# A hand-ordered attention-and-gated-MLP block on one core: w_phi loaded first, nearly all loads on one queue, and a new order of work

## The chip, the core and the metric

The kernel runs on one core of one Trainium2 chip. The time is the device time of one execution in microseconds (us). Three runs of the kernel before give 271.66 to 272.04 us, with a median of 271.83 us.

## What is computed

Two pre-normalised layers over one sequence of 2048 rows and 640 columns, in bf16. The first is linear attention with 32 heads of 20 columns and a softmax feature map; the second is a gated product of two projections.

```python
x = A_x
h = x + _A_ref(_layernorm(x), A_wqkv, A_w_phi, A_wo)
h2 = h + _B_ref(_layernorm(h), B_w_gate, B_w_up, B_w_down)

# _A_ref
pq, pk = q @ w_phi[head], k @ w_phi[head]
phi_q = concat([softmax(pq), softmax(-pq)]);  phi_k = concat([softmax(pk), softmax(-pk)])
kv = phi_k^T v;  z = sum(phi_k);  o = (phi_q kv) / (phi_q z + 1e-6);  return o @ wo
# _B_ref
return ((x @ w_gate) * (x @ w_up)) @ w_down
```

## The kernel before

The 2048 rows are 16 tiles t of 128 rows. Every step of the program is a named operation, recorded by `G.op(engine, name, ...)`, and the table `PLAN` gives each name a key, an alternative engine and its buffer slots. `arrange` sorts by the key, so each engine's instruction list is written out in full by the table. `emit` adds the semaphore waits. An engine runs its list strictly in order: what waits holds up all that stands behind it. The names used below are these.

- Loads (line 285): `x0` to `x14` bring x (x4, x6, x8 and so on bring two tiles, 320 KB), `w5` brings w_phi (25 KB), `wk0` to `wk4` and `wv0` to `wv4` the key and value parts of wqkv (160 KB each). `wo`, `wd`, `wg`, `wu` bring the later weights, mostly 480 KB. `wqt0` to `wqt4` (line 309) bring the query part of wqkv by DMA transposes. All are issued by SP, or by ACT.
- Preparation of the weights: `zero` (DVE) and `warm` (PE, lines 367 and 372, products of zeros), `Ph0` to `Ph2` (POOL, line 380: w_phi spread out in the tensor Phi), `WT` (PE transposes of `wk`, line 392) with their copies `WTe`, and the folds `F1_i` and `F0_i` (PE, line 411: w_phi folded into the key and the query weights) with their copies `Fe` into the tensor Wp. All such copies out of PSUM have line 251.
- Normalisation of tile t: `L1s` (DVE, lines 428 and 429) and `L1a` (431) take statistics, `L1l` and `L1e` (ACT, 436 and 439) make the scale, `L1n` its product with the mean, and `xn` (453) the normalised tile. It is transposed by PE for tiles 0 and 1 (`xt`, line 462) and by the DMA queue of SP for the others (line 471).
- Projections (PE, line 482): `V`, `K` and `Q` of tile t. The first two tiles are cut into five parts, `K0_0` to `K0_4`, so that each part waits for one piece of the folded weights alone. Features: `Kx`, `Qx` (ACT, exponentials), `Ks`, `Qs` (DVE, lines 498 and 556, sums), `Kr`, `Ke`, `Qr`, `Qe` (ACT, logarithm and exponential), `Kn`, `Qn` (POOL, lines 518 and 570, scaling), and `Qb` (line 563), the subtraction of the two logarithms of a query's sums, on DVE or POOL. `qT` is the DMA transpose of the query features.
- Attention: `KV` (PE, line 526) sums up over all tiles, `N` (588) is the numerator, `dd`, `rd`, `o` (DVE) divide, `oT` is a DMA transpose, and `O` (625) multiplies with wo. `h` (DVE, 631) adds x. `hc` and the DMA transpose `hT` prepare the second layer.
- Second layer: `U` (PE, line 668) the two projections in blocks of rows, `g` (ACT) and `u` (DVE) their product, `D` (687) the product with w_down, `y` (DVE, 699) the sum with h, and the store.

The kernel's own filler on PE is set by two lines, which say how many zero products there are, and which of them have to precede the first transposes:

```python
NFILL = 14
wall = [G.by["warm%d" % k] for k in range(8)]
```

Of the kernel before, what the change touches and what calls it, by code (L numbers as in the profile page):

```python
# [47 lines left out]
NFILL = 14  # L48
# [5 lines left out]
x1:0.78:1 ekz:0.78 x0:0.78 zero:0.91 id0:1.014 warm0:1.127 id1:1.252 x3:1.26:1 wk3:1.26:1 warm1:1.345 va1:1.496 warm2:1.564 w5:1.74:1 warm3:1.782 warm4:2.001  # L54
warm5:2.219 wk0:2.22:1 eps:2.326 gl0:2.357 warm6:2.437 gla:2.518 warm7:2.656 wk4:2.7:1 glb:2.822 warm8:2.874::0 warm9:3.093 wk1:3.18 warm10:3.311 warm11:3.529
wk2:3.66:1 L1s1:3.725 warm12:3.748 warm13:3.966 x4:4.14 warm14:4.185 warm15:4.403 L1s0:4.512 wv1:4.62 warm16:4.621 warm17:4.84 wv0:5.1:1 L1a1:5.299 L1s3:5.408
WT3:5.446::1 L1l1:5.532 wv2:5.58:1 Ph2:5.775 L1e1:5.858 warm18:5.902 warm19:6.011 wv3:6.06 WTe3:6.1:1 warm20:6.12 L1a0:6.195 xn1:6.304::0 Ph1:6.369 x2:6.54
WT0:6.546::2 L1l0:6.685 Ph0:6.761 L1a3:6.834 xt1:6.971::3 wv4:7.02:1 WTe0:7.023:1 L1l3:7.067 L1e0:7.249 WT4:7.25::4 L1e3:7.393 xte1:7.486 xn0:7.487::1 x6:7.5
L1n3:7.673 WT1:7.746::5 phz:7.897 WTe4:8.017:1 warm21:8.025 F1_0:8.134::6 WTe1:8.223:1 xn3:8.425::2 F1_3:8.453::0 WT2:8.772::2 Fe1_0:8.808:1 xt0:9.051::3
xt3:9.063 WTe2:9.249:1 F1_1:9.33::4 Fe1_3:9.392 F1_4:9.649::6 xte0:9.657:1 Fe1_1:9.976 L1s4:10.065 F1_2:10.153::0 x8:10.373 K0_0:10.472::2 Fe1_2:10.67:1  # L60
K0_1:10.743 L1s5:10.852 wqt4:10.853 K1_0:11.014::4 Fe1_4:11.254:1 K1_1:11.285 K1_2:11.556 L1a4:11.639 L1a5:11.762 V1_0:11.827::0 L1l4:11.995 K1_3:12.098
wqt1:12.163 L1s2:12.225 L1e4:12.321 V0_0:12.369::6 K1_4:12.64 V1_1:12.911 L1n5:13.012:1 Kx1_0:13.11::0 V0_1:13.182 xn5:13.296::3 V0_2:13.453 Kx1_1:13.694
V0_3:13.724 L1a2:13.826 xt5:13.934 L1s7:13.935 V0_4:13.995 K0_2:14.266 L1l2:14.278 K0_3:14.537 L1e2:14.604 Ve0:14.697::0 Ks1:14.722::0 V1_2:14.808 L1n2:14.884
V1_3:15.079 Sz:15.108 wqt0:15.244 xn2:15.281:1:0 L1n4:15.287 V1_4:15.35 K3:15.621::4 L1s6:16.115 Kr1:16.234 Ke1:16.525 xt2:16.554 x12:16.671:1 Kn1:16.859
K0_4:16.977 L1a6:17.025 xn4:17.134::1 Kx3_0:17.177::1 V3:17.248::6 L1s8:17.664 Kx3_1:17.761 wqt2:17.864 Ve1:18.345::1 L1a7:18.451 L1s9:18.56 K5:18.604::4
L1l6:18.929 xt4:19.174 L1e6:19.255 Ks3:19.347::1 Ve3:19.348::2 L1n7:19.535 L1n6:19.759 Kx0_0:19.932::2 V5:19.96::0 rqz:19.983 wqt3:20.484 Kx0_1:20.516
xn7:20.74::2 Kx5_0:21.1::3 xn6:21.27::3 K2:21.316::6 Kx5_1:21.684 L1a8:21.8 xt6:21.908 L1a9:21.909 Ks0:22.018::2 Kr3:22.268 Ke3:22.559 V2:22.672::2
Ve5:22.705::3 Kn3:22.893 xt7:23.218 Kx2_0:23.289::4 Ks5:23.411::3 Kx2_1:23.873 V4:24.028::4 Ve2:24.457::4 x10:24.528 L1s12:24.804 x14:25.008 L1l8:25.041
L1e8:25.367 F0_0:25.384::0 Kr0:25.46 wg2:25.488 Ks2:25.591::0 L1n8:25.647 F0_2:25.703::6 Ke0:25.751 L1n9:25.871 Ve4:25.897::5 wg0:25.968 V6:26.022::2 Kn0:26.095
Fe0_0:26.481 L1s13:26.984 xn9:27.065:1:0 F0_4:27.378::4 K4:27.697::0 Kr5:27.88 Fe0_4:27.895:1 xt9:28.018 Ve6:28.026::6 mk0:28.408 mk1:28.572 Kr2:28.61  # L70
L1s11:28.635 Ke2:28.901 Fe0_2:29.047 KV0:29.053::4,5 Kn2:29.235 wd1:29.328 KV1:29.386 L1s10:29.422 Kx4_0:29.631::2 K7:29.719::2 L1s14:30.209 Kx4_1:30.215
F0_3:31.075::6 L1a14:31.119 L1a10:31.228 Kx7_0:31.275::0 xn8:31.337::1 V7:31.394::0 smz:31.548 Fe0_3:31.859 L1a11:31.867 xt8:31.975 Ks4:31.976::1 Kx7_1:32.443
KV2:32.75 Ke5:33.027 KV3:33.083 L1l10:33.173 wg1:33.285 L1s15:33.369 F0_1:33.416::6 L1e10:33.499 K6:33.735::2 L1n11:33.779 Fe0_1:33.933 Kn5:34.003
# [16 lines left out]
Ke14:68.065 Qx13_0:68.211::1 V15:68.695::0 Qx13_1:68.821 Ve12:69.431::3 Qs13:69.616 Kn14:69.675 V14:70.051::2 Ve15:70.251::6 Qs10:71.051 KV11:71.407  # L90
Ve14:71.607::7 KV12:71.74 KV13:72.073 Qe4:72.191 Qr13:72.31::3 KV14:72.406 Qn4:72.498 Qr10:72.604::0 KV15:72.739 Q6:73.072::6 KVe0:73.27 Qb13:73.763 KVe1:73.859
N0:74.439::0 Qx6_0:74.637::4 N2:74.772::2 qT4:74.963::2 dd0:74.97::0 Q7:75.105::4 rd0:75.185 Qx6_1:75.247 dd2:75.475::1 o0:75.599::0 rl2:75.857 rd2:76.211
Qe13:76.391 oT0:76.467::0 N1:76.472::6 o2:76.536::1 Qx7_0:76.67::2 Qn13:76.698 Q11:76.805::0 Qx7_1:77.28 dd1:77.291::0 rd1:77.506 oT2:77.777::1 o1:77.92::2
Qb10:77.963 N9:78.172::2 Qe10:78.238 Qx11_0:78.37::5 Q8:78.505::4 dd9:78.703::0 rd9:78.918 Qx11_1:78.98 qT13:79.087::5 Qs7:79.208 N3:79.872::6 Qx8_0:80.07::0
Q14:80.205::0 oT1:80.577::2 o9:80.643::0 Qx8_1:80.68 Qr7:81.29::2 dd3:81.398::0 N5:81.572::4 rd3:81.613 Qb7:81.634 oT9:81.887::3 O0:81.905::2 Qe7:81.909
o3:82.027::1 Qn7:82.216 dd5:82.782::0 O2:83.263::6 oT3:83.455::0 h0:83.462 Qx14_0:83.997::1 Qs6:84.282 Qx14_1:84.607 O1:84.723::2 qT7:84.765::0 hc0:85.217::2
h2:85.717 Qr6:85.935::1 N4:86.081::0 hT0:86.255 Qb6:86.279 h1:86.537 Qe6:86.554 rl5:86.673 O9:86.684::6 Qn6:86.861 rd5:87.027 hc1:87.481:1:1 o5:87.934::2
# [140 lines left out]
def build_graph():  # L238
    G = Graph()
# [134 lines left out]
    wall = [G.by["warm%d" % k] for k in range(8)]  # L374
# [554 lines left out]
```

## Time and profile before

| | |
|---|---|
| median of three runs | 271.83 us (271.66 to 272.04) |
| span of the profiled execution | 270.1 us |
| its own whole time | not shown apart; the runs lie 1.6 to 1.9 us above its span |
| PE busy | 264.2 us, 98% of the span |
| DVE, ACT, POOL busy | 160.0, 124.0 and 71.3 us |
| granted TensorE clock | 1.00 |

The span runs from the first to the last instruction of the core. What the runs take beyond it lies before and after the program, and the two versions have it alike. PE is busy nearly throughout, so what a change is worth is what it does to the few places where PE isn't, or waits at the start and the end.

### The profile page before, as it was taken

The page shows a single profiled execution, that of the slowest core. Times are in us where ns is not written, and L with a number is a line of the kernel's source. Part 1 is how long each engine was busy: PE and PEld are TensorE (multiplying, and loading weights), DVE is VectorE, ACT ScalarE, POOL GpSimd, SP SyncE. Part 2 cuts the span into 40 slices and gives each one's busy share as a digit, 9 for nine tenths or more (in the row PEclk, how much of TensorE's full clock was granted, in tenths as well). Part 3 has the DMA queues.
Part 4 walks back from the last instruction along what each step waited for, and adds up shares of the span by engine and source line. Part 5 has one row for each costly group of instructions (what it writes and reads, how often), then busy time and mean ns, then how long its engine had stood idle before and what let it go on. Part 6 is the DMA issues. An engine that isn't in the chain of part 4 may idle for free.

```text
span 270.1 us, 5186 instructions
## 1 busy us (share of the span) xinstructions
PE 264.2 (98%) x2092; PEld 177.9 (66%) x2105; DVE 160.0 (59%) x294; ACT 124.0 (46%) x316; POOL 71.3 (26%) x89
## 2 busy tenths in 40 slices
PE   7999999999999999999999999999999999999996
PEld 5777877777777788665556667765554476544774
DVE  4999799978988998577664253332342311423432
ACT  3899999988786382763540051222122300023000
POOL 4255689999923222205000000000000000000000
PEclk9999999999999999999999999999999999999999
DMA  7997995999958897973950001260200001100011
GB/s 200 318 168 136 249 222 129 302 183 245 204 106 143 163 126 149 140 123 64 171 93 2 0 0 36 57 106 1 73 12 2 0 0 51 49 1 0 27 49 61
DMA packets 71752, 28.09 MB, mean 104 GB/s; under 512 B 59056, under 2 KB 71728, under 8 KB 71728
## 3 DMA queue, kind: packets, MB, share of 16 engines
q1 hardware_dynamic: 71168, 27.10, 49.9%
q10 hardware_dynamic: 560, 0.66, 0.8%
q8 instruction: 16, 0.26, 0.4%
q14 instruction: 8, 0.07, 0.1%
HBM read 11.00 MB, written 2.62 MB: 50 GB/s over the span
## 4 chain that ended last, share of the span: by engine, by line
PE 90%; DMA 5%; DVE 2%; ACT 1%; issue 1%; SPq 1%; DVEq 0%
PE ps L668 36%; PE ps L482 24%; PE ps L687 19%; PE ps L625 6%; DMA scratch<-ph 2%; PE ps L526 2%; PE ps L588 2%; DMA Wp<-o 2%; DMA x_all<-in_A_x_dram 1%; PE ps L411 1%; SPq L653 1%; DVE st L428 0%; ACT Wp L251 0%; DVE st L429 0%; DVE ev L676 0%
## 5 line engine op out<-in xcount | busy, mean ns | idle before, releaser
L668 PE MATMUL ps<-xnT,Wgu 128*128 128x512 bf16 (+1 forms) x587 | 106.0, 335 | 0.7
L668 PEld LDWEIGHTS ps<-xnT,Wgu 128*128 128x128 bf16 x600 | 58.3, 98 | 43.4
L673 ACT ACTIVATE gt<-ps 128x512 bf16<-128x512 f32 (+1 forms) x60 | 29.7, 509 | 100.9 <-PE ps L668 62.9
L482 PE MATMUL ps<-Wp,xnT 128*128 128x320 bf16 (+1 forms) x480 | 68.6, 298 | 0.0
L482 PEld LDWEIGHTS ps<-Wp,xnT 128*128 128x128 bf16 x480 | 45.5, 97 | 17.2 <-issue 0.2
L676 DVE TENSOR_TENSOR ev<-ps,gt 128x512 bf16<-128x512 f32 (+1 forms) x60 | 33.6, 579 | 36.5 <-PE ps L668 27.8
L687 PE MATMUL ps<-Wd,ev 128*128 128x320 bf16 (+2 forms) x396 | 53.9, 295 | 0.0
L687 PEld LDWEIGHTS ps<-Wd,ev 128*128 128x128 bf16 x396 | 38.1, 98 | 15.3 <-DVE ev L676 0.2
L699 DVE SCALAR_TENSOR_TENSOR Wp<-ps,rs,x_all 128x640 bf16<-128x640 f32 (+3 forms) x18 | 14.6, 810 | 49.3 <-PE ps L687 49.1
L518 POOL TENSOR_TENSOR ek<-ek,SR 128x1280 bf16<-128x1280 bf16 x16 | 37.5, 2358 | 5.2 <-ACT SR L503 5.1
L551 ACT ACTIVATE ph<-ps 128x600 bf16<-128x600 f32 x32 | 21.4, 680 | 8.0 <-PE ps L482 6.9
L556 DVE TENSOR_REDUCE S<-ph 128x66 f32<-128x1320 bf16 x16 | 23.9, 1516 | 1.8 <-ACT ph L553 1.8
L625 PE MATMUL ps<-Wo,Wp 128*128 128x320 bf16 x160 | 23.9, 299 | 0.2
L498 DVE TENSOR_REDUCE SR<-ek 128x64 f32<-128x1280 bf16 x16 | 23.3, 1468 | 1.0 <-ACT ek L494 1.0
L570 POOL TENSOR_TENSOR ph<-ph,RQ 128x660 bf16<-128x660 bf16 x16 | 20.7, 1308 | 8.9 <-ACT RQ L566 8.9
L646 POOL TENSOR_SCALAR ln<-mv 128x1 f32<-128x1 f32 x12 | 2.3, 191 | 75.7 <-ACT ek L642 75.1
L494 ACT ACTIVATE ek<-ps 128x640 bf16<-128x640 f32 x32 | 21.2, 719 | 2.2 <-PE ps L482 1.5
L625 PEld LDWEIGHTS ps<-Wo,Wp 128*128 128x128 bf16 x160 | 15.3, 98 | 6.4 <-DMA Wp<-o 0.4
L631 DVE SCALAR_TENSOR_TENSOR x_all<-ps,x_all 128x640 bf16<-128x640 f32 x16 | 13.1, 821 | 6.4 <-PE ps L625 6.4
L615 DVE TENSOR_TENSOR o<-ps,sm 128x660 bf16<-128x660 f32 x16 | 13.4, 840 | 0.9 <-ACT sm L608 0.6
L642 ACT ACTIVATE ek<-x_all,mv 128x640 bf16<-128x640 bf16 x16 | 13.1, 821 | 0.0
L251 ACT ACTIVATE ev<-ps 128x640 bf16<-128x640 f32 x16 | 11.2, 704 | 1.1 <-PE ps L482 1.1
(69 smaller groups left out, 161.9 us busy)
## 6 DMA issues: line engine op xcount, KB each, us to landing
out_dram<-Wp SPq DMA_DIRECT2D x15, 160.0 KB, 1.8
Wgu<-in_B_w_gate_dram SPq DMA_DIRECT2D x4, 480.0 KB, 6.2
Wd<-in_B_w_down_dram SPq DMA_DIRECT2D x4, 480.0 KB, 4.7
Wgu<-in_B_w_up_dram SPq DMA_DIRECT2D x4, 480.0 KB, 5.6
x_all<-in_A_x_dram SPq DMA_DIRECT2D x5, 320.0 KB, 5.0
Wp<-in_A_wqkv_dram SPq DMA_DIRECT2D x5, 160.0 KB, 4.7
ev<-in_A_wqkv_dram SPq DMA_DIRECT2D x4, 160.0 KB, 4.2
x_all<-in_A_x_dram SPq DMA_DIRECT2D x3, 160.0 KB, 3.2
```

Of the source, the lines that this page charges most:

```text
L482: ins = e.matmul(pb(b, hb)[:, 0:n1 - n0], lhsT=T["xnT"][:, NC - 1 - c, P * t:P * (t + 1)], rhs=T["Wp"][:, POS[kind], c, n0:n1], start=(c = ...
L494: G.op("act", "%sx%d_%d" % (nm, t, s), lambda e, s=s, b=b, ek=ek: e.activation(out=T["ek"][:, ek.slots[0], 0:2 * D].rearrange("p (b h s f) ...
L498: G.op("dve", "%ss%d" % (nm, t), lambda e, ek=ek, sr=sr: e.tensor_reduce(out=T["SR"][:, sr.slots[0], 0, :], in_=T["ek"][:, ek.slots[0], 0: ...
L518: G.op("pool", "Kn%d" % t, lambda e, eng, ek=ek, sr=sr: e.tensor_tensor(out=T["ek"][:, ek.slots[0], 0:2 * D].rearrange("p (h f) -> p h f", ...
L551: e.activation(out=v[:, 0:10].rearrange("p (b g) j f -> p b g j f", b=2), in_=pp(b, 0, 300).rearrange("p b (g j f) -> p b g j f", j=3, f=D ...
L556: G.op("dve", "Qs%d" % t, lambda e, t=t, ph=ph: e.tensor_reduce(out=T["S"][:, t, 0:66].rearrange("p (g k) -> p g k", k=6), in_=pv(ph).rear ...
L570: return e.tensor_tensor(out=v, in0=v, in1=T["RQ"][:, rq.slots[0], 1, 0:33].rearrange("p (g j) -> p g j", j=3).unsqueeze(3).to_broadcast([ ...
L625: ins = e.matmul(pb(b, hb)[:, 0:320], lhsT=T["oT"][:, oT.slots[0], c, :], rhs=T["Wo"][:, c, 320 * hb:320 * (hb + 1)], start=(c == 0), stop ...
L668: ins = e.matmul(pb(b)[:, 0:n], lhsT=T["Wgu"][:, gu, c, P * ft:P * (ft + 1)], rhs=T["xnT"][:, NC - 1 - c, o0:o0 + n], start=(c == 0), stop ...
L673: G.op("act", "g%d_%d" % (bi, ft), lambda e, pg=pg, gt=gt, n=n: e.activation(out=T["gt"][:, gt.slots[0], 0:n], in_=pb(pg)[:, 0:n], func=AF ...
L676: o_ = G.op("dve", "u%d_%d" % (bi, ft), lambda e, pu=pu, gt=gt, hh=hh, ft=ft, n=n: e.tensor_tensor(out=T["hh"][:, hh.slots[0], ft, 0:n], i ...
L687: ins = e.matmul(pb(b, hb)[:, 0:w], lhsT=T["hh"][:, hh.slots[0], ft, P * tt:P * (tt + 1)], rhs=T["Wd"][:, ft, c0 + w * hb:c0 + w * (hb + 1 ...
```

## The change

The table is a new one throughout; its keys are now places in a list, 0 to 1027, and no longer times. Besides it two lines change:

```diff
-NFILL = 14
+NFILL = 12
-    wall = [G.by["warm%d" % k] for k in range(8)]
+    wall = [G.by["warm%d" % k] for k in range(16)]
```

What the new table says, beside the order itself (a last `:1` chooses the other engine):

```diff
-x1:0.78:1 ekz:0.78 x0:0.78 ... x3:1.26:1 wk3:1.26:1 ... w5:1.74:1
+zero:0 x0:1:1 ... w5:3:1 ... x3:7:1 wk0:8 ... wk1:12 ... x1:18
-... x12:16.671:1
+... x14:191 ... x12:195
-Qb9:55.781:1 ... Qb2:61.591:1 ... Qb4:67.516:1
+Qb2:369 ... Qb9:416 ... Qb4:457
```

`w5` becomes the first load of SP's queue. ACT issues `x0` and `wk0` (before: `x1`, `wk3`, and later `x12`); all other loads are SP's. All sixteen `Qb` are on POOL; before, three were on DVE. Sixteen zero products are made to precede the first transpose; there are 20 in all, where there were 22. Also moved are four of the copies `Ve` (from ACT to DVE), five of the normalisations `hc` (from DVE to ACT), and some small ones.

The first place is the head of SP's queue, its loads up to the first transpose. In the kernel before, x_all is x, w5 is w_phi, ev is `wk` and Wp is `wv`:

```order
L285 DMA x_all<-in_A_x_dram 128x640 x2
L285 DMA w5<-in_A_w_phi_dram 128x5x20
L285 DMA ev<-in_A_wqkv_dram 128x640 x4
L285 DMA x_all<-in_A_x_dram 128x2x640
L285 DMA Wp<-in_A_wqkv_dram 128x640 x4
```

And now:

```order
L263 DMA w5<-in_A_w_phi_dram 128x5x20
L263 DMA x_all<-in_A_x_dram 128x640
L263 DMA ev<-in_A_wqkv_dram 128x640
L263 DMA x_all<-in_A_x_dram 128x640
L263 DMA ev<-in_A_wqkv_dram 128x640 x2
L263 DMA Wp<-in_A_wqkv_dram 128x640
```

w_phi moved ahead of the x tiles 3 and 1 and of every `wk` that SP loads. DVE's list changes with it: before, it takes the statistics of tiles 1, 0 and 3 and then normalises tile 1; now it takes those of tiles 0 and 3, normalises tile 0, and takes those of tile 1 after that.

The second place is SP's queue from the transpose of tile 3 to the last query weights. L471 (now L449) is the transpose of a normalised tile, L309 (now L287) that of a piece of query weights, L285 (now L263) a load of two tiles of x. Before:

```order
L471 DMA_TRANSPOSE xnT<-xn 128x5x128
L285 DMA x_all<-in_A_x_dram 128x2x640
L309 DMA_TRANSPOSE scratch<-in_A_wqkv_dram 128x1x640 x2
L471 DMA_TRANSPOSE xnT<-xn 128x5x128
L309 DMA_TRANSPOSE scratch<-in_A_wqkv_dram 128x1x640
L471 DMA_TRANSPOSE xnT<-xn 128x5x128
L309 DMA_TRANSPOSE scratch<-in_A_wqkv_dram 128x1x640
L471 DMA_TRANSPOSE xnT<-xn 128x5x128
L309 DMA_TRANSPOSE scratch<-in_A_wqkv_dram 128x1x640
```

And now:

```order
L449 DMA_TRANSPOSE xnT<-xn 128x5x128
L287 DMA_TRANSPOSE scratch<-in_A_wqkv_dram 128x1x640 x2
L449 DMA_TRANSPOSE xnT<-xn 128x5x128
L263 DMA x_all<-in_A_x_dram 128x2x640
L449 DMA_TRANSPOSE xnT<-xn 128x5x128
L263 DMA x_all<-in_A_x_dram 128x2x640
L449 DMA_TRANSPOSE xnT<-xn 128x5x128
L287 DMA_TRANSPOSE scratch<-in_A_wqkv_dram 128x1x640 x3
```

Three of the five pieces of query weights now stand behind all three transposes of tiles 2, 5 and 4 and behind two loads that lie between these.

The third place is PE's list where the products with wo begin. L588 (now L566) is a numerator `N`, L625 (now L603) is `O`. Before, `N5`, then `O0`, `O2`, `O1`, then `N4`, then `O9` and `O3`:

```order
L588 MATMUL ps<-KVm,scratch 128x63 x10
L588 MATMUL ps<-KVm,scratch 128x42
L625 MATMUL ps<-Wo,Wp 128x320 x30
L588 MATMUL ps<-KVm,scratch 128x63 x10
L588 MATMUL ps<-KVm,scratch 128x42
L625 MATMUL ps<-Wo,Wp 128x320 x20
```

And now, `O0` and `O2`, `N5`, `O1` and `O3`, `N4`:

```order
L603 MATMUL ps<-Wo,Wp 128x320 x20
L566 MATMUL ps<-KVm,scratch 128x63 x10
L566 MATMUL ps<-KVm,scratch 128x42
L603 MATMUL ps<-Wo,Wp 128x320 x20
L566 MATMUL ps<-KVm,scratch 128x63 x10
L566 MATMUL ps<-KVm,scratch 128x42
```

The projection `Q14` (ten products) moved from ahead of this piece to behind it, and of the `O` only four stand here, in the order in which their transposes are issued; `O9` follows after `Q14`.

More of the change, by code (lines that the diff above doesn't have):

```diff
@@ L53 @@
 for _t in """
[L54 to L73, printed above, removed]
@@ L90 @@
[L90 to L97, printed above, removed]
@@ L142 @@
[L142 to L145 removed]
+zero:0 x0:1:1 id0:2 w5:3:1 eps:4 warm0:5 gl0:6 x3:7:1 wk0:8 warm1:9 warm2:10 gla:11 wk1:12 warm3:13 id1:14 warm4:15 warm5:16 glb:17 x1:18 warm6:19 ekz:20
@@ new lines @@
+qT4:466::1 Qx6_1:467 Q7:468::0 rd0:469 dd2:470::0 o0:471::0 Qr13:472::3 rl2:473 Qb13:474 rd2:475 Qb10:476 o2:477::1 N1:478::4 Qx7_0:479::2 Q11:480::2
+oT0:481::0 dd1:482::0 Qx7_1:483 rd1:484 o1:485::2 N9:486::6 oT2:487::1 Qx11_0:488::5 N3:489::0 dd9:490::0 Q8:491::4 rd9:492 Qx11_1:493 dd3:494::3 rd3:495
+oT1:496::2 Qe13:497 o3:498::0 Qn13:499 O0:500::2 Qx8_0:501::0 oT3:502::3 o9:503::1 Qx8_1:504 O2:505::0 Qe10:506 h0:507 oT9:508::0 Qs7:509 hc0:510::3 N5:511::2
+O1:512::4 qT13:513::2 h2:514 Qr7:515::3 Qb7:516 Qn10:517 O3:518::6 h1:519 hT0:520 hc1:521::2 N4:522::0 h3:523 Q14:524::4 L2q1:525 hT1:526 dd5:527::2
```

129 lines of the change are left out of this document (65 added, 64 removed).

## The prediction

> **What bounds the kernel now.** I read the page first, then the busy time by stages, then the chain of waits, and then the queue of SP in order of time.
>
> ```profile
> PE 264.2 (98%) x2092; PEld 177.9 (66%) x2105; DVE 160.0 (59%) x294; ACT 124.0 (46%) x316; POOL 71.3 (26%) x89
> PE 90%; DMA 5%; DVE 2%; ACT 1%; issue 1%; SPq 1%; DVEq 0%
> ```
>
> PE is busy for 98% of the span and is 90% of the chain that ended last. The stages (start and end, length, then busy time of PE, PEld, DVE, ACT, POOL) show where the rest is:
>
> ```profile
> 5.00:10.50 5.50, 4.47 (x70) 3.84 (x69) 5.36 (x16) 4.60 (x12) 2.65 (x6) 1.00 1.02 342
> 10.50:80.00 69.50, 69.50 (x704) 52.07 (x701) 62.62 (x96) 62.45 (x169) 51.64 (x44) 1.00 0.96 197
> 80.00:90.00 10.00, 9.76 (x97) 6.91 (x96) 8.95 (x17) 4.89 (x17) 4.35 (x5) 1.00 0.85 150
> 110.00:120.00 10.00, 9.46 (x73) 5.99 (x74) 6.56 (x13) 6.51 (x18) 0.25 (x2) 1.00 1.01 140
> 120.00:260.00 140.00, 139.41 (x873) 84.05 (x881) 54.66 (x112) 32.81 (x68) 4.72 (x13) 1.00 0.18 38
> 260.00:270.10 10.10, 7.67 (x68) 5.74 (x66) 3.01 (x6) 0.00 (x0) 0.00 (x0) 1.00 0.17 57
> ```
>
> From 10.5 to 80 us PE has no idle time at all, though the three other engines are 74 to 90% busy there. It loses 0.24 us in 80 to 90, 0.54 in 110 to 120 and 0.59, in crumbs, in 120 to 260. The clock is 1.00 everywhere. The change neither adds nor removes a real product, so it can act only through the start, these 1.37 us, and new waits. The tail keeps its last three groups of products and their stores in the same order: 0. The chain's first pieces (start, us, what) show what sets the start:
>
> ```profile
> 0.83 3.06 DMA x_all<-in_A_x_dram
> 3.91 0.49 DVE st L428
> 4.41 0.39 DVE st L429
> 5.59 0.11 DVE mv L431
> 6.55 0.47 DVE xn L453
> 7.17 0.29 ACT ln L436
> 7.47 0.23 ACT rs L439 x2
> 8.89 1.20 ACT Wp L251 x2
> 10.22 0.48 PE ps L411 x6
> 10.70 14.95 PE ps L482 x110
> 25.65 0.64 PE ps L411 x12
> ```
>
> It is a load of x, then DVE's statistics of three tiles (0.39 us each half), then ACT's copies of folded weights. The stream of projections starts at 10.70 us, and from there 110 products run gapless to the first fold of query weights at 25.65.
>
> **The change part by part: the start.** I need when the loads land. These are the rows of w_phi and of the single loads (KB each, us to landing), of two issues on the queues, and of POOL's use of w_phi:
>
> ```profile
> 1.26 0.45 ACTq L285 DMA_DIRECT2D ev<-in_A_wqkv_dram  x1
> 1.72 0.43 SPq L285 DMA_DIRECT2D w<-in_A_w_phi_dram  x1
> x_all<-in_A_x_dram SPq DMA_DIRECT2D x3, 160.0 KB, 3.2
> ev<-in_A_wqkv_dram ACTq DMA_DIRECT2D x1, 160.0 KB, 3.6
> w<-in_A_w_phi_dram SPq DMA_DIRECT2D x1, 25.0 KB, 4.3
> 6.13 1.68 POOL L380 TENSOR_TENSOR Phi<-w,GL 128x280 bf16<-128x280 bf16 x3 [2.47 <-DMA w<-in_A_w_phi_dram]
> ```
>
> w_phi is 25 KB and yet lands at 1.72 + 4.3 = 6.0 us, 1.2 after the 160 KB that ACT had issued just before it (1.26 + 3.6 = 4.9). So it holds the queue for up to 1.2 us; I take 0.7 and keep 0.3 to 1.2. As first load it should land by about 0.8 + 4.3 = 5.1, and POOL's 1.68 us then end at 6.8, not 7.8. Tile 0 comes by ACT and lands at 3.9 as tile 1 does now. Tile 3 is issued second (1.25) and lands at 1.25 + 3.2 + 0.7 = 5.1; tile 1 is fourth, at 5.9 or so.
>
> DVE then takes tile 0 (two halves, 0.78, and 0.11: to 4.8), ACT makes its scale meanwhile, DVE takes tile 3 from 5.1 to 5.9 and normalises tile 0 to 6.4, where the chain now has 6.55 + 0.47 = 7.02. Tile 1's statistics end at 7.3. Two copies, the other two normalisations (0.5 each) and three further copies follow; their price is this row's 470 ns, the chain's 0.39 when they follow each other:
>
> ```profile
> L251 DVE COPY scratch<-ps 128x640 bf16<-128x640 bf16 x3 | 1.4, 470 | 0.0
> ```
>
> That brings DVE to 10.6. ACT's scale of tile 1 is ready at about 8.3 (7.3, 0.52 from the chain, some passing on, and tile 3's between). Its first copy of folded weights ends at 8.9, tile 3's scale at 9.1, and the second copy, the one for which the first projection waits, at 9.7. The first projection can start at 9.95. One fold (0.32, half of the chain's 0.64 for two) is still among the projections that follow, so the stream stands as if begun at 10.25 instead of 10.70: **-0.45 us**. With tile 3 and tile 1 0.5 us later, and w_phi's full 1.2, it is nothing or +0.3; I keep -0.6 to +0.3.
>
> The Trainium skill speaks against this edit: "DMA: Bandwidth & Descriptors", Specifications, gives 512 B as the least transfer for line rate, and w_phi comes in pieces of 40 B. The slow landing of the 25 KB agrees. Going by that alone, w_phi first would push all x loads back by its whole slot, which is the last rival below.
>
> The zero products: before, the first transpose stands behind 18 of them in a row (8 and 10), and it does so after the change; the sixteen are no new work, and the two dropped ones stood in gaps where PE waited. 0, and at the most 0.2 either way.
>
> **The middle: SP's queue.** Rows of the queue in order of time (start, us on the queue), and the times to landing of lines 471 and of 309, the query weights:
>
> ```profile
> 14.59 1.28 SPq L471 DMA_TRANSPOSE xnT<-xn  x1
> 21.17 1.27 SPq L309 DMA_TRANSPOSE scratch<-in_A_wqkv_dram  x1
> 25.13 1.14 SPq L285 DMA_DIRECT2D x_all<-in_A_x_dram  x2
> 28.21 3.10 SPq L471 DMA_TRANSPOSE xnT<-xn  x1
> ...
> DMA to landing us min/median/max: 2.6/3.3/6.9
> ...
> DMA to landing us min/median/max: 3.2/4.2/5.0
> ```
>
> Now the last query weights are issued at 21.17 and PE's first query fold runs at 25.65. After the change tile 2 is normalised by DVE. After 10.6 come three pairs of statistics (0.78 each), small ones of 0.1 and the normalisation, so it is ready at about 14.0 and its transpose is issued at 14.1. To the last query weights stand five transposes of 1.28 and two loads of 0.57, with 0.04 between: 7.8, so 21.9. They land 3.2 to 5.0 later, at 25.1 to 26.9. PE needs them at 10.25 + 14.95 = 25.2, for the same 110 products stand ahead of the first query fold. The wait is -0.1 to 1.7; I take a landing time of 3.9, between the least, when little else was in flight, and the median: **+0.6 us**. Behind the fold on PE stand all keys, values and queries to come, so a wait there is lost for good.
>
> Next on this queue is tile 9's transpose, which now took 3.10 us on the queue and, as the largest, 6.9 to land: 35.1. Four loads stood ahead of it (1,600 KB); now three do (1,120 KB). By this row DVE has work of about 14.4 us between tile 2's and tile 9's normalisation:
>
> ```profile
> L498 DVE TENSOR_REDUCE SR<-ek 128x64 f32<-128x1280 bf16 x16 | 23.3, 1468 | 1.0 <-ACT ek L494 1.0
> ```
>
> That is five such sums (7.0), five pairs of statistics (3.9), four normalisations (2.0) and 1.5 of small ones: tile 9 is issued at 28.5 and lands at 31.1 to 35.4. PE comes to its key projection after five folds, four projections of 1.36 and four `KV` of 0.34 (the chain's rows for 10 and 11 products), 8.4 us behind the first fold: at 33.6, or 34.2 with the wait above. That is a wait of 0 to 1.2; I take **+0.3**.
>
> The load `x12`, moved from ACT's queue to SP's, adds 0.57 there. The Trainium skill ("DMA: Bandwidth & Descriptors", Issuing engines are not separate DMA queues) says that loads of several queues share the same DMA engines and only the issue time is saved; a landing of up to 5.0 for query weights beside ACT's load agrees. By it the middle costs no less than I take.
>
> **The rest.** The two PE waits that are more than crumbs are these (the chain, and the timeline of PE):
>
> ```profile
> 84.39 4.20 DMA Wp<-o
> 88.63 1.53 PE ps L625 x10
> 113.00 0.51 PE L588 MATMUL ps<-KVm,scratch 128*128 128x63 bf16 x11 [0.44 <-DMA scratch<-ph]
> ```
>
> The first is `O3`, which waits for its transpose; that stands last of `oT0`, `oT2`, a query transpose, `oT1` and `oT9`. In the new queue it stands ahead of `oT9` and of the query transpose, some 2.7 us earlier at 1.28 and more each, so I take the wait as gone. The second is `N15`, which now comes some forty `U` products later. Together **-0.78**; nothing but the crumbs is late next, since PE has `U` products to run in both places. At the least they come back elsewhere: 0.
>
> The three subtractions moved from DVE to POOL free DVE of two long ones (start, us), each beside a POOL scaling:
>
> ```profile
> 61.94 0.90 DVE L563 TENSOR_TENSOR RQ<-RQ 128x32 f32<-128x32 f32 x1 [0.20 <-ACT RQ L559]
> 67.79 2.21 DVE L563 TENSOR_TENSOR RQ<-RQ 128x32 f32<-128x32 f32 x1
> ```
>
> On POOL they cost 0.24 each. PE is gapless in that stage, so this is worth 0; the cover is PE's own queue of projections, and if that failed it would be up to 3. The four `Ve` and five `hc` that change engine are hidden likewise: 0.
>
> **Sum.** -0.45 + 0.6 + 0.3 - 0.78 = -0.33. The profiled span of 270.1 becomes 269.8; the runs' median lies 1.7 above the span, and that part is untouched: 271.83 - 0.33 = **271.5 us**.
>
> **The rivals.** *A clean middle:* the query weights land in 3.3 and tile 9 in the median 3.3. For it: 21.9 + 3.3 = 25.2 is just in time. Against: two more loads in between. It gives 271.83 - 0.45 - 0.78 = 270.6. *SP's queue becomes the bound* (the other side): one of its transposes stalls as the 3.10 one does, the query weights land at 26.9 and tile 9 at 36 or later; price 1.7 + 1.2 = 2.9, so 271.83 - 0.45 - 0.78 + 2.9 = 273.5. It decides from 1.8 us of waits on (1.23 + 0.54). For it: that row, and loads now between transposes. Against: the other transposes quoted took 1.27 and 1.28. *w_phi's small pieces delay x:* tiles 3 and 1 land 0.5 later and the start is +0.3 rather than -0.45: 272.25. That the sixteen zero products do nothing is part of every case.
>
> **How the numbers follow.** About 0.2% (0.54 us) can be told from no change. The forecast (270.9 to 272.3) has 0.40: 0.13 of it faster, 0.25 the same, 0.02 slower. A clean middle 0.20: 0.19 faster, 0.01 the same. SP's queue 0.28: 0.27 slower, 0.01 the same. w_phi 0.12: 0.06 the same, 0.06 slower. Together 0.32 faster, 0.33 the same, 0.35 slower. The range from 270.4 to 273.4 takes in all of the cases but the farther half of SP's queue and the edge of the clean one.
>
> **What would show it.** In the profile after, the first projection at 9.8 to 10.1 us with POOL's w_phi product ending by 6.9 shows the start right; at 10.5 or later it is wrong. The first query fold with an idle time ended by a DMA of query weights shows the middle; no such wait there or at tile 9's key projection means a clean middle. No `O` and no `N` that waits for a transpose in 75 to 125 us shows the 0.78. A span over 271.5 with PE gapless from 10 to 36 us would mean that I missed the place altogether.

## The result and the profile after

The changed kernel takes 272.21 us in the median of 20 runs, the kernel before 271.49 us in 20 runs on the same chip: a ratio of 1.0031, with an interval of 1.0017 to 1.0045. It is 0.7 to 0.8 us slower, where 271.5 us and a gain of 0.33 were forecast. (The three runs of before that the forecast started from lay 0.34 above this median.) The profiled execution of before is one of those three, at 271.83; that of the changed kernel took 272.19. So the two profiles differ by 0.36, half of the 0.72 between the medians, and only this half can be looked for in them. One run of an experiment below, at 276.08 with a granted clock of 0.994 (`mid_act`), is in no ratio.

The page of the profile after has the same outline, but the chain of work has more DMA and more of SP's queue in it:

```profile
PE 264.4 (98%) x2103; PEld 177.5 (66%) x2103; DVE 157.0 (58%) x296; ACT 123.4 (46%) x317; POOL 70.7 (26%) x86
PE 83%; DMA 6%; DVE 4%; ACT 3%; SPq 2%; POOL 1%; issue 1%; DVEq 0%
```

The busy time by stages, cut at the same times in both (length, then PE, PEld, DVE, ACT, POOL). After:

```profile
25.00:37.00 12.00, 11.27 (x135) 8.70 (x133) 11.44 (x27) 10.56 (x27) 9.87 (x7) 1.00 0.97 223
75.00:85.00 10.00, 9.67 (x123) 7.29 (x121) 8.12 (x18) 7.25 (x22) 2.96 (x4) 1.00 0.87 144
85.00:100.00 15.00, 15.00 (x137) 11.63 (x136) 13.46 (x25) 9.26 (x28) 2.02 (x4) 1.00 0.94 177
100.00:115.00 15.00, 14.84 (x127) 10.82 (x126) 8.96 (x23) 7.14 (x22) 5.74 (x8) 1.00 0.70 104
115.00:260.00 145.00, 145.00 (x946) 88.00 (x945) 58.31 (x124) 38.68 (x86) 5.37 (x10) 1.00 0.23 50
```

Before:

```profile
25.00:37.00 12.00, 12.00 (x143) 9.44 (x142) 10.05 (x24) 11.28 (x27) 8.78 (x11) 1.00 0.99 229
75.00:85.00 10.00, 10.00 (x123) 7.53 (x120) 8.81 (x19) 8.08 (x27) 3.05 (x4) 1.00 0.75 139
85.00:100.00 15.00, 14.76 (x143) 11.55 (x141) 14.24 (x28) 8.78 (x27) 4.06 (x6) 1.00 0.81 148
100.00:115.00 15.00, 14.51 (x148) 11.26 (x147) 10.74 (x24) 8.14 (x26) 3.73 (x6) 1.00 0.98 136
115.00:260.00 145.00, 144.36 (x903) 87.11 (x913) 58.51 (x118) 35.42 (x76) 4.96 (x14) 1.00 0.20 41
```

The two waits of before are gone (0.24 in 85 to 100, 0.49 in 100 to 115), and three places have lost time instead: 0.73 in 25 to 37, 0.33 in 75 to 85 and 0.16 in 100 to 115. That is 1.22 for 0.73. PE's timeline names them (start, us, what, idle time ahead and its releaser), between the first projections and the last products:

```profile
9.81 1.25 PE L460 MATMUL ps<-Wp,xnT 128*128 128x320 bf16 x8
25.83 0.80 PE L389 MATMUL ps<-Phi,scratch 128*128 128x140 bf16 x12 [0.55 <-ACT SR L481]
34.56 3.72 PE L460 MATMUL ps<-Wp,xnT 128*128 128x320 bf16 x26 [0.19 <-DMA xnT<-xn]
79.66 0.85 PE L566 MATMUL ps<-KVm,scratch 128*128 128x63 bf16 x22 [0.33 <-DMA scratch<-ph]
110.05 6.20 PE L646 MATMUL ps<-xnT,Wgu 128*128 128x512 bf16 x28 [0.16 <-issue]
254.78 13.23 PE L665 MATMUL ps<-Wd,ev 128*128 128x320 bf16 x108
```

These are the query fold `F0_4`, the key projection `K9`, `N9` (the numerator of tile 9) and `U1_3_0`. The same rows of before for the two ends:

```profile
10.54 1.66 PE L482 MATMUL ps<-Wp,xnT 128*128 128x320 bf16 x11
254.77 12.90 PE L687 MATMUL ps<-Wd,ev 128*128 128x320 bf16 x105
```

The first projection starts 0.73 earlier; one fold (0.32) now comes behind it, so 0.41 is gained. The last product ends at 268.01 for 267.67. So the gain of the start, 0.41, and the 0.73 of the removed waits were outweighed. The stages add up to +0.08 (-0.41 + 1.22 - 0.73) and the ends to +0.34; the 0.26 between are not put down to a place. The other half of the measured change, 0.38, is not in these two profiles at all.

How the waits came about is read from SP's queue (start, us on the queue), with the times of the query weights' transposes below it (ns on the queue, first and last start; then us to landing), and from POOL:

```profile
16.11 0.58 SPq L263 DMA_DIRECT2D x_all<-in_A_x_dram  x1
16.74 1.21 SPq L449 DMA_TRANSPOSE xnT<-xn  x1
17.99 0.58 SPq L263 DMA_DIRECT2D x_all<-in_A_x_dram  x1
18.62 1.20 SPq L449 DMA_TRANSPOSE xnT<-xn  x1
19.86 3.90 SPq L287 DMA_TRANSPOSE scratch<-in_A_wqkv_dram  x3
...
27.60 0.47 SPq L263 DMA_DIRECT2D Wo<-in_A_wo_dram  x1
29.50 3.12 SPq L449 DMA_TRANSPOSE xnT<-xn  x2
...
74.39 3.14 SPq L553 DMA_TRANSPOSE scratch<-ph  x2
...
96.21 0.58 SPq L263 DMA_DIRECT2D Wd<-in_B_w_down_dram  x1
101.06 1.38 SPq L553 DMA_TRANSPOSE scratch<-ph  x1
...
L287 SPq DMA_TRANSPOSE scratch<-in_A_wqkv_dram x5: 1271/1272/2109, 11.3 to 22.5; - x5
DMA to landing us min/median/max: 3.1/3.8/4.6
```

```profile
70.74 2.35 POOL L496 TENSOR_TENSOR ek<-ek,SR 128x1280 bf16<-128x1280 bf16 x1 [0.32 <-ACT SR L481]
73.06 1.31 POOL L548 TENSOR_TENSOR ph<-ph,RQ 128x660 bf16<-128x660 bf16 x1
```

The last query weights (`wqt2`) are issued at 22.5, behind the loads `x10` and `x8`, and took the least of the five landing times, 3.1; 22.5 + 3.1 = 25.6, and the fold that needs them starts at 25.83, 0.2 later. (The row names an ACT operation that was merely the last event in sight: the fold doesn't read `SR`. In the experiments below it starts 0.2 to 0.3 after the last query weights land each time: issued 22.4, landed in 3.6, fold at 26.25 in `wo2_late`; 22.3, 5.0 and 27.55 in `x12_act`, where the row names the DMA.) `N9` waits for `qT9`, issued at 74.39: tile 9's queries stand behind tile 14's keys (2.35) in POOL's list and are scaled until 74.37. It landed 5.2 later, at 79.6, and `N9` starts at 79.66. That the order on POOL is the cause is read from the rows; no run changes it. `hT5`, for which `U1_3_0` waits, stands behind `qT7`, which held the queue from 96.8 to 101.06 waiting for its input.

### The profile page after: what moved, and what is told of

The parts are those of the page before. It is cut to its first block, busy times and chain, and to the rows that moved or that the text cites. A ratio compares the mean times of both kernels' runs of the same rounds, so it can differ in the third digit from the quotient of the medians.

```text
span 270.5 us, 5196 instructions
## 1 busy us (share of the span) xinstructions
PE 264.4 (98%) x2103; PEld 177.5 (66%) x2103; DVE 157.0 (58%) x296; ACT 123.4 (46%) x317; POOL 70.7 (26%) x86
## 4 chain that ended last, share of the span: by engine, by line
PE 83%; DMA 6%; DVE 4%; ACT 3%; SPq 2%; POOL 1%; issue 1%; DVEq 0%
PE ps L646 39%; PE ps L665 19%; PE ps L460 14%; PE ps L603 8%; SPq L263 2%; DMA scratch<-ph 2%; DMA xnT<-xn 2%; DMA x_all<-in_A_x_dram 2%; PE ps L566 2%; ACT ek L472 1%; DVE SR L476 1%; POOL ek L496 1%; PE ps L504 1%; ACT ev L229 1%; DVE st L407 1%
## 5 line engine op out<-in xcount | busy, mean ns | idle before, releaser
L646 PE MATMUL ps<-xnT,Wgu 128*128 128x512 bf16 (+1 forms) x600 | 108.1, 336 | 0.2 <-issue 0.2
L548 POOL TENSOR_TENSOR ph<-ph,RQ 128x660 bf16<-128x660 bf16 x16 | 20.9, 1311 | 28.6 <-ACT RQ L544 28.5
L603 PE MATMUL ps<-Wo,Wp 128*128 128x320 bf16 x160 | 23.5, 299 | 0.0
L529 ACT ACTIVATE ph<-ps 128x600 bf16<-128x600 f32 x32 | 21.4, 683 | 4.0 <-PE ps L460 2.6
L472 ACT ACTIVATE ek<-ps 128x640 bf16<-128x640 f32 x32 | 21.4, 708 | 1.7 <-PE ps L460 1.3
L603 PEld LDWEIGHTS ps<-Wo,Wp 128*128 128x128 bf16 x160 | 15.6, 98 | 6.6 <-issue 0.2
L624 POOL TENSOR_SCALAR ln<-mv 128x1 f32<-128x1 f32 x6 | 1.2, 192 | 62.3 <-ACT ek L620 62.0
L618 ACT ACTIVATE xn<-x_all,mv 128x640 bf16<-128x640 bf16 x10 | 8.1, 822 | 6.1 <-DVE x_all L609 6.1
```

The source lines that it names most:

```text
L472: G.op("act", "%sx%d_%d" % (nm, t, s), lambda e, s=s, b=b, ek=ek: e.activation(out=T["ek"][:, ek.slots[0], 0:2 * D].rearrange("p (b h s f) ...
L529: e.activation(out=v[:, 0:10].rearrange("p (b g) j f -> p b g j f", b=2), in_=pp(b, 0, 300).rearrange("p b (g j f) -> p b g j f", j=3, f=D ...
L548: return e.tensor_tensor(out=v, in0=v, in1=T["RQ"][:, rq.slots[0], 1, 0:33].rearrange("p (g j) -> p g j", j=3).unsqueeze(3).to_broadcast([ ...
L603: ins = e.matmul(pb(b, hb)[:, 0:320], lhsT=T["oT"][:, oT.slots[0], c, :], rhs=T["Wo"][:, c, 320 * hb:320 * (hb + 1)], start=(c == 0), stop ...
L646: ins = e.matmul(pb(b)[:, 0:n], lhsT=T["Wgu"][:, gu, c, P * ft:P * (ft + 1)], rhs=T["xnT"][:, NC - 1 - c, o0:o0 + n], start=(c == 0), stop ...
```

## The experiments

Each is the changed kernel with entries of `PLAN` replaced, unless it says otherwise. Ratios are against the kernel before on the same chip; the changed kernel in the second group had 1.0051 (1.0035 to 1.0067). Only its own repetition, `mid_act`, `wo2_late` and `n9_late` belong to that group; the others have only the kernel before beside them. The 1.0051 rests on six runs and the 1.0031 on twenty, and their intervals overlap, so a gain of 0.3 to 0.5 us on the changed kernel cannot be told from the ratios: there the profiles say which wait is gone, and not what it was worth.

**The changed kernel again.** 

> The changed kernel once more, as the zero for the others of this group. Theory (new waits of PE): 0.4 to 1.1 us slower than before, with PE idle ahead of F0_4 (0.7), K9 (0.36) and N9 (0.5). Rival (the difference is chance of one comparison): within 0.3 us of before, and the waits differ from profile to profile.

 It took 272.89 against 271.61. The same places wait (the fold 0.29, `K9` 0.4, `N9` 0.33). But its start was another one; PE's timeline of this run:

```profile
2.80 2.34 PE L350 MATMUL ps<-ev 128*128 128x256 bf16 x10
5.89 0.71 PE L370 MATMUL ps<-ident,ev 128*128 128x128 bf16 x5 [0.75 <-DMA ev<-in_A_wqkv_dram]
7.97 1.81 PE L370 MATMUL ps<-ident,ev 128*128 128x128 bf16 x15
11.48 0.70 PE L460 MATMUL ps<-Wp,xnT 128*128 128x320 bf16 x4
```

and of the first profile of the same kernel:

```profile
2.80 1.83 PE L350 MATMUL ps<-ev 128*128 128x256 bf16 x10
5.42 0.45 PE L370 MATMUL ps<-ident,ev 128*128 128x128 bf16 x5 [0.79 <-DMA ev<-in_A_wqkv_dram]
7.14 1.00 PE L370 MATMUL ps<-ident,ev 128*128 128x128 bf16 x15
```

Fifteen transposes take 1.81 here and 1.00 there: for 1.8 us PE took 120 ns for one where it takes 67, and the first projection starts at 11.48 and not 9.81, 1.67 later. I call this a start at half speed; its slow products last until about 10.5 us.

**Two loads on ACT's queue.**
```diff
-x10:135 x8:146
+x10:135:1 x8:146:1
```


> The loads x10 and x8 go to ACT's queue, so that SP's queue carries transposes alone ahead of the last query weights. Theory (SP's queue serves in order, and two loads among the transposes make the last query weights late): wqt2 lands 1.2 to 2 us earlier, F0_4 waits no more, xt9 lands earlier too and K9 waits no more; 0.7 to 1.07 us faster than the changed kernel. Rival (loads and transposes share the same DMA engines, whichever queue issued them): wqt2 lands at most 0.3 us earlier, F0_4 waits 0.4 or more, and the time changes by less than 0.4.

 271.54 us, 0.9998 (0.9982 to 1.0014): no loss against before can be told. It is 1.35 us less than the six runs of the changed kernel beside it; by the ratio of the twenty runs it would be 0.9. The last query weights are issued at 21.4 (22.5 before the edit) and land in 3.7, at 25.1; the fold at 25.77 and `K9` at 34.16 do not wait, and PE is busy for 12.00 of 12.00 in 25 to 37. The waits that are gone are 0.69 together in that kernel's profile, so they need not be the whole gain: two of its six runs, one of them the profiled one with the half-speed start, lie at 273.50 and 273.56, the others at 272.61 to 272.89. ACT issued the two loads at 14.40 and 17.39, ahead of the last three of the query weights' transposes. A smaller wait has come up, for tile 2's transpose:

```profile
18.97 6.97 PE L462 MATMUL ps<-Wp,xnT 128*128 128x320 bf16 x50 [0.27 <-DMA xnT<-xn]
```

**The load x12 on ACT's queue,** as in the kernel before.
```diff
-x12:195
+x12:160.5:1
```


> The load x12 alone goes back to ACT's queue, as in the kernel before. Theory (each load ahead of tile 9's transpose on SP's queue makes it land later): that transpose is issued 0.5 us earlier and lands 0.5 to 1.3 earlier, K9's wait of 0.36 goes, F0_4's stays; 0.36 us faster than the changed kernel. Rival (the queue doesn't matter): K9 waits as long.

 274.48 us, 1.0083 (1.0053 to 1.0113). The median lies between two sets: five runs at 273.19 to 273.89, the profiled one among them, and five at 275.07 to 275.86. `K9` waits no more, but it comes 1.7 later behind the fold, which waits for 2.17, so this doesn't show that x12 was what held it up:

```profile
27.55 0.80 PE L390 MATMUL ps<-Phi,scratch 128*128 128x140 bf16 x12 [2.17 <-DMA scratch<-in_A_wqkv_dram]
...
L288 SPq DMA_TRANSPOSE scratch<-in_A_wqkv_dram x5: 1272/1281/1874, 11.4 to 22.3; - x5
DMA to landing us min/median/max: 3.5/5.0/5.9
```

The query weights were issued no later (22.3) and the last of them in 5.0 instead of 3.1 (the median of the five: 5.0 instead of 3.8). ACT issued the load at 19.99, among them, and this is the one edit. So a load delays transposes from the other queue too, and what counts is when it is issued. Neither theory had said so.

**wo2 behind tile 9's transpose.**
```diff
-wo2:201
+wo2:214.5
```


> The load wo2 (480 KB) is issued behind the transpose of tile 9 and not ahead of it. Theory: xt9 lands 0.7 to 1.3 us earlier, K9's wait of 0.36 goes, F0_4's 0.7 stays; 0.36 us faster than the changed kernel. Rival (tile 9 is late because its normalisation is late, or because x14 and x12 are still under way): xt9 lands within 0.3 us of before, K9 waits on, time unchanged.

 272.52 us, 1.0038 (1.0023 to 1.0053). `K9` waits no more: tile 9's transpose, issued at 29.9, landed in 2.9, where it took 5.0 from 29.5 behind wo2. That is the theory's mechanism. The time is 0.37 under the changed kernel's beside it, which is within the overlapping intervals, so a gain is not shown; the fold's idle time is 0.75.

**N9 behind Q8.**
```diff
-N9:486::6 dd9:490::0
+N9:491.5::6 dd9:491.6::0
```


> PE takes the projection Q8 (1.36 us) ahead of N9 and not behind it. Theory: N9's wait of 0.50 for the transposed query features of tile 9 is covered by Q8, nothing behind it comes late, 0.50 us faster than the changed kernel. Rival (the wait moves on: the divisions and transposes behind N9 come 1.36 us later, and O9 or another product waits in its place): 0 to 0.2 us faster, with a new wait between 78 and 95 us.

 274.16 us, 1.0097 (1.0078 to 1.0115). The theory fell: `N9` waits no more, and `Q8` and `O2` wait in its place for divisions on DVE:

```profile
80.10 1.54 PE L462 MATMUL ps<-Wp,xnT 128*128 128x300 bf16 x10 [0.21 <-DVE o L595]
84.15 1.52 PE L605 MATMUL ps<-Wo,Wp 128*128 128x320 bf16 x10 [0.81 <-DVE o L595]
```

**N3 ahead of N9,** with the divisions in the same order.
```diff
-N9:486::6 dd9:490::0 rd9:492
+N9:489.5::6 dd9:495.2::0 rd9:495.3
```


> PE takes N3 (0.34 us, its inputs ready) ahead of N9 and not behind it, and DVE takes tile 3's division ahead of tile 9's. Theory: of N9's wait of 0.50, 0.34 is covered, and what follows does not come later, unlike in the run that put the longer Q8 ahead: 0.3 us faster than the changed kernel. Rival (o9 and oT9 come later and O9 or O2 waits): time unchanged.

 272.38 us, 1.0021 (1.0003 to 1.0039). PE is busy for 10.00 of 10.00 in 75 to 85, and nothing waits in its place. The wait is covered; the changed kernel was not run beside it, and 1.0021 is not told from its 1.0031.

**qT7 behind four transposes.**
```diff
-qT7:591::2 hT5:620
+hT5:615.5 qT7:616::2
```


> On SP's queue the transpose qT7 stands behind hT3, oT13, hT4 and hT5 and not ahead of them. Theory (qT7 waits for the scaling of tile 7 on POOL and holds the queue for 4 us, so hT5 lands too late for U1_3_0): hT5 lands 1 us or more earlier, the 0.31 us ahead of U1_3_0 go, 0.31 us faster than the changed kernel. Rival (hT5 is late because its input is late, or N7 and what hangs on it then waits for qT7): no gain, a wait at N7 or another product near 110 us.

 278.86 us, 1.0264 (1.0231 to 1.0298): a buffer that neither theory had thought of. The exponentials of tile 15 write where `qT7` reads, so ACT stood still for 4.75, and with it the factor that a `U` needs. ACT's and PE's rows:

```profile
110.89 0.67 ACT L531 ACTIVATE ph<-ps 128x600 bf16<-128x600 f32 x1 [4.75 <-DMA scratch<-ph]
...
112.65 3.06 PE L648 MATMUL ps<-xnT,Wgu 128*128 128x256 bf16 x15 [4.51 <-ACT gt L653]
```

The wait cost more than itself: the granted clock is 0.50 from 113 to 116 us, and the fifteen products behind it take 204 ns each, where the twenty of the same size ahead of it take 117.

**Only hT3 ahead of qT7.**
```diff
-hT3:600
+hT3:590.5
```


> Only the transpose hT3 moves ahead of qT7 on SP's queue; its input is ready 5 us before qT7's. Nothing else waits longer for it, unlike in the run that moved qT7 behind four transposes. Theory: hT5 is issued 1.3 us earlier, lands before 109, the wait of 0.25 to 0.38 us ahead of U1_3_0 goes and no wait comes in its place: 0.3 us faster than the changed kernel. Rival: U1_3_0 waits for a factor of block 0 or another product waits, time unchanged.

 272.37 us, 1.0016 (0.9997 to 1.0035). PE is busy for 15.00 of 15.00 in 100 to 115: the wait is gone, as expected. As with `n3_first`, the ratio is not told from the changed kernel's.

**w_phi fourth.**
```diff
-w5:3:1
+w5:18.5:1
```


> w_phi is loaded fourth on SP's queue (behind x3, wk1 and x1) and not first. Theory A (the earlier start of the projections comes from w_phi): POOL's products end 1.5 us or more later, the first projection starts 0.3 to 0.6 us later, time +0.3 to +0.6 against the changed kernel. Theory B (in the changed kernel w_phi was done 1.8 us before the first fold that needs it, so the gain came from the order of the x loads and of DVE's work): x3 and x1 land up to 0.5 earlier, the first projection starts within 0.15 us or earlier, time -0.3 to +0.1.

 273.76 us, 1.0065 (1.0039 to 1.0091). The first fold waits 0.97 for POOL's products and the first projection starts at 10.74, not 9.81. The sign is theory A's, though tile 3's load did land earlier. That is 0.93 at the start; by the ratios the run is 0.4 to 0.9 us over the changed kernel, with an interval that overlaps that of the twenty runs.

**w_phi first in the kernel before.**
```diff
-w5:1.74:1
+w5:0.05:1
```


> The kernel before, with w_phi first on SP's queue and nothing else changed. Theory A (w_phi first is what moves the start forward): the first projection starts 0.2 to 0.5 us earlier than before. Theory B (the start hangs on the first x tile and DVE's statistics): x0 is issued 0.45 us later and held up by the small pieces, the first projection starts 0.3 to 1.2 us later and the time is up by as much.

 271.77 us, 1.0006 (0.9989 to 1.0023); the first projection starts at 10.65 for 10.54. Both theories fell: by itself the edit does nothing that can be told. In before's order the first fold starts at 8.04, and w_phi is in time either way. It is the new order of folds that needs it first.

**Subtractions back on DVE.**
```diff
-Qb2:369 Qb9:416 Qb4:457
+Qb2:369:1 Qb9:416:1 Qb4:457:1
```


> The subtractions of tiles 2, 9 and 4 go back from POOL to DVE, in their new places. Theory (the cover, PE's own queue of projections, holds): no change within 0.2 us, though single ones may take 0.9 to 2.2 us beside POOL's scalings. Rival (POOL's queue sets qT9, so less work on POOL lands qT9 earlier): N9's wait of 0.50 shrinks by 0.24 or more, 0.2 to 0.5 us faster than the changed kernel. Third possibility: DVE's long ones delay Qn9, N9 waits longer, slower by up to 1.

 272.89 us, 1.0048 (1.0031 to 1.0065), the changed kernel's own ratio. `N9`'s wait did not shrink. The cover holds.

**The zero products.** Ten in all:
```diff
-NFILL = 12
+NFILL = 2
-wall = [G.by["warm%d" % k] for k in range(16)]
+wall = [G.by["warm%d" % k] for k in range(10)]
```


> The changed kernel with 10 zero products in all, ahead of the first transpose, and not 18 and 2. Theory (a gap ahead of the first transpose while PE is not yet at full speed leaves it at half speed until 10 us): the gap is 1.7 us or longer, every start is at half speed, the first 25 transposes take 0.71 to 0.74 us for five, the first projection starts 1.4 us later and all runs are 1 to 1.6 us slower than the changed kernel. Rival (zero products do nothing): no change.

 274.53 us, 1.0089 (1.0061 to 1.0117), all six runs at 273.87 or more. PE's rows:

```profile
2.80 0.63 PE L350 MATMUL ps<-ev 128*128 128x256 bf16 x2
5.42 0.72 PE L370 MATMUL ps<-ident,ev 128*128 128x128 bf16 x5 [1.98 <-DMA ev<-in_A_wqkv_dram]
7.65 1.81 PE L370 MATMUL ps<-ident,ev 128*128 128x128 bf16 x15
```

Twenty-one in a row ahead of the first transpose (`warm18` to `warm20` moved or added there, two more behind it, `wall` to match). 

> 21 zero products in a row ahead of the first transpose and not 18 (23 in all and not 20), so that PE has less idle time before the key weights land. Theory (PE's speed in the first 10 us depends on whether it was busy without a gap; in one of eight profiles of this order the transposes after the gap ran at half speed until 10.5 us, at a cost of 1.4 us): no profile and no run with such a start, median 0 to 0.3 us faster than the changed kernel and a smaller spread. Rival (the speed doesn't depend on the gap): no change, or +0.2 where the zero products hold up WT1.

 272.36 us, 1.0002 (0.9986 to 1.0018), highest run 273.13. Ahead of the transposes is no idle time, and the fifteen take 1.00. The waits of the changed kernel are all still there (0.95 in 25 to 37, `N9` 0.43), and yet its ratio is as near to 1 as that of `mid_act`, which removes waits and leaves the zero products alone. So the ratios do not separate how much of the loss was waits and how much starts at half speed.

The same in the kernel before, three more where it waited 0.70. 

> The kernel before with three more zero products ahead of the transposes of wk0, where its PE waited 0.70 us. Theory (before has some half-speed starts too): its runs above 272.5 go, median 0 to 0.3 us faster than before. Rival (before, whose first transposes already run at 4.9 us, has none): no change within 0.2.

 271.33 us, 0.9983 (0.9965 to 1.0001). No run is over 272.21, where 4 of the 23 runs of before beside them are over 272.5. This speaks for such starts in before too; no profile of it shows one.

**Together.** x10 and x8 on ACT's queue, hT3 early, N3 first. 

> The loads x10 and x8 on ACT's queue, hT3 ahead of qT7, and N3 ahead of N9 together. Theory (the waits are independent and lie in a row on PE): the gains add, 1.35 + 0.3 + 0.3, so 0.4 to 0.7 us faster than the kernel before. Rival (what is taken away in one place is lost at the next late transfer): no better than the run with the two loads alone, equal to before.

 271.94 us, 1.0004 (0.9987 to 1.0022): seven runs at 271.39 to 271.99 and five at 272.56 to 273.19, and the profiled one had the half-speed start (fifteen transposes in 1.81, after an idle time of 0.73). With the 21 zero products: 

> combo1 with 21 zero products in a row ahead of the first transpose. Theory: the upper group of combo1's runs (five of twelve at 272.6 to 273.2, the others at 271.4 to 272.0) goes, median 271.4 to 271.8, highest run below 272.5. Rival (the two groups have another cause): runs above 272.5 in the same share.

 271.47 us, 0.9986 (0.9968 to 1.0004), highest run 272.35. The upper group is gone. No version of the new order has a lower ratio. That it beats before is not shown, and before with its three more zero products has 0.9983.

With x10 at 138.5 and x8 at 160.5: 

> combo3 with x10 issued one step later on ACT's queue, and x8 behind the tile 1 work. Theory (x10, issued by ACT just ahead of tile 2's transpose, takes the DMA engines from it): the transpose of tile 2 lands 1 us earlier, K2's wait of 0.44 goes, 0.4 us faster than combo3. Rival (tile 2's transpose is late because tile 2 is normalised late, or x10 now delays another transpose): a wait of 0.3 or more remains at K2 or V2.

 273.23 us, 1.0041 (1.0022 to 1.0060), for x8 now came late to DVE, and `KV0` waited 0.97 for a fold's copy behind it. The wait for tile 2's transpose, which this run was to remove, stayed (0.55), so the rival was right:

```profile
25.29 0.49 DVE L417 BATCH_NORM_STATS2 st<-x_all 128x6 f32<-128x320 bf16 x1 [2.61 <-DMA x_all<-in_A_x_dram]
```

With wv2 ahead of x4: 

> combo3 with wv2 (160 KB) issued ahead of x4 (320 KB). Theory: wv2 lands 0.9 us earlier, the wait of 0.5 to 0.7 at V1_2 goes, 0.3 to 0.6 us faster than combo3 and 0.5 to 1.0 faster than before, with the interval below 1. Rival (x4 now late, tile 4 or 5 late in its place): equal to combo3.

 271.82 us, 0.9987 (0.9967 to 1.0007). The wait for wv2 is gone, one of 0.29 for a tile's transpose came up, and the ratio is combo3's: no gain.

## Why the prediction was wrong

**The start, -0.45:** 0.41 in the first profile, the first projection at 9.81 within the 9.8 to 10.1 named. The number is right, in part by luck, for the way to it was another. w_phi landed in 2.6 us and not 4.3, so POOL was done by 5.2, not 6.8 (the page's row of the load, and POOL's timeline):

```profile
w<-in_A_w_phi_dram SPq DMA_DIRECT2D x1, 25.0 KB, 2.6
...
3.47 1.68 POOL L358 TENSOR_TENSOR Phi<-w,GL 128x280 bf16<-128x280 bf16 x3
```

I had the first projection wait for ACT's second copy of folded weights, at 9.7. In the profile PE does not wait for it: it runs without a gap from 6.53, and the projection comes 3.0 behind the first fold, which starts at 6.82. The same 3.0 stand between them in `mid_act` (7.07 and 10.07), `qb_dve` (6.77 and 9.77) and `w5_fourth` (7.75 and 10.74). So in this order the start is set by when the first fold can run. The reason was half right: w_phi first is needed by the new order (`w5_fourth`) and worth nothing alone (`before_w5first`). What the Trainium skill says against it in "DMA: Bandwidth & Descriptors", Specifications, did not decide: the 25 KB in front landed in less time than before. For the zero products I had "0, and at the most 0.2", and that was mis-sized: I had left out PE's speed at the start. A half-speed start costs 1.3 to 1.7 us (the first projection at 11.35 and 11.48), and two of the eleven profiles with this start have one. Whether the change made these more frequent is not shown.

**The middle, +0.6 and +0.3:** 0.55 and 0.19 idle, at the two places named and for the transfers named. Right, with two slips that cancel at the fold: the last query weights were issued at 22.5 and not 21.9, and landed in 3.1 and not 3.9. Tile 9's transpose was issued at 29.5 (28.5 forecast) and landed at 34.5, within the 31.1 to 35.4.

**The removed waits, -0.78, is the step that failed.** They are gone, but "nothing but the crumbs is late next" did not hold: 0.33 came up at `N9` and 0.16 at `U1_3_0`. I had looked only at the products that wait in before, with the transposes ahead of those, and not at every `N`, `O` and first `U` of a block in the new order. `qT9` moved from a place with 8.2 us to spare (issued at 63.3, it landed at 70.3, for an `N9` that started at 78.5) to one with none. The net is -0.24 in the windows, not -0.78. (The two waits were 0.73 in these windows. The -0.78 counted the whole 0.54 lost in 110 to 120 for `N15`, whose own row has 0.44.) Both new waits are covered in the profiles of `n3_first` and `ht3_early`; that the time follows is not shown, for the intervals of 1.0021 and 1.0016 overlap the changed kernel's.

This step makes 0.54 of the miss. Between the two profiles the kernel moved by +0.34 at its ends for the -0.33 forecast, a miss of 0.67: 0.54 from this step, 0.04 from the start, -0.17 from the middle, and the 0.26 put down to no place. The medians moved by 0.38 more. For both of these remainders the cause stays open.

**The crumbs, 0.59 in 120 to 260, were no loss.** The two kernels have the same 600 `U` products. Before's page counts 587:

```profile
L668 PE MATMUL ps<-xnT,Wgu 128*128 128x512 bf16 (+1 forms) x587 | 106.0, 335 | 0.7
```

The page after counts all, and PE is busy for 145.00 of 145.00 there:

```profile
L646 PE MATMUL ps<-xnT,Wgu 128*128 128x512 bf16 (+1 forms) x600 | 108.1, 336 | 0.2 <-issue 0.2
```

The order of before, changed only ahead of its first projection, is busy for 145.00 of 145.00 in 115 to 260 in the profiles of `before_w5first` and `before_fill`, with 914 products on record there and not 903. So the crumbs go with missing records.

**The rivals.** "SP's queue becomes the bound" named the mechanism of the middle: `mid_act` takes two loads off the queue, the waits there go, and it is 0.5% faster than the changed kernel's six runs in the same group. That these waits are all of the loss is not shown, for `fill21` keeps them and is level with before too. For the price I thought of a stalled transpose, at 2.9 us; it was loads ahead of transposes and transposes ahead of others whose inputs were ready. And "one queue" was not the fault as such: the moved load x12 does more harm on ACT's queue.

**The subtractions, 0:** right (`qb_dve`).

## What to carry to other kernels

When an order is rewritten, list for every product its latest input and the time to spare, not only for those that wait now: a removed wait pays only up to the next one in line. A transfer is placed by when it is issued among the others; another queue saves its time on the first one (`mid_act`) but does not by itself take it out of their way (`x12_act`). A moved transfer also moves the release of the buffer it reads, and an engine far off may stand still for that.

## What the runs showed of the hardware

PE starts at half speed, and when it comes to full speed varies from run to run. Ten zero products took 2.34 us in some profiles and 1.74 to 2.14 in others; at 2.34 each takes 0.23, and a product of the same size later in the span takes 0.11 (35 of them in 3.98 from 105.57 in `after`). Where the ten took 2.34 and PE then idled for 0.73 or 0.75 us (`combo1`, `after_again`), the first transposes came at half speed and it stayed so until about 10.5 us. With the same 2.34 and an idle time of 0.51 (`n3_first`, `x12_act`) or 0.69 (`mid_act`) the transposes came at full speed (the fifteen in 1.00); with 0.26 (`n9_late`), 0.38 (`ht3_early`) and 0.43 (`wo2_late`) the first five were still slow and the fifteen were not. Where the ten took less, full speed had come before the gap, and 0.74 (`qt7_late`) or 0.79 (`after`) did no harm either. With an idle time of 1.98 (`zero10`) it was at half speed again. No run shows where the limit lies, or that the length of the gap alone decides. The Trainium skill, "TensorE: Matmul & The Clock Gate", What's actually happening, says that the clock is raised after a window of sustained activity, and that the windows run freely and do not begin with the kernel. The two speeds and the varying moment agree with that.

The granted clock of the profile reads 1.00 in these stages all the same, so at the start the speed has to be read from the durations of like products. Later in the span it does show: 0.50 from 113 to 116 us in `qt7_late`, behind an idle time of 4.51. That stretch, with 0.79 in the us behind it, lacks 1.7 us of clock in 276.7, which makes 0.994, the mean on record for that run. Four of the ten runs of `x12_act`, with its idle time of 2.17, and three of the six of `w5_fourth` have 0.994 too; that they have such a stretch is an inference, for their profiles are of runs at 1.00.
